# Last two stores of GpSimd on SyncE, the last eviction in two halves, and the last row block stored as two halves

## The chip, the cores and the metric

One core of one Trainium2 chip. The metric is the device time of one execution in microseconds, as the median of several runs.

## The reference

Two heads read inputs of 2048 rows by 1024 columns and their results stand side by side in an output of 2048 x 2048, in bf16.

```
# head A (columns 0 to 1023)
k_shift = sum over t<4 of k[l-(3-t)] * shift_k[:, 3-t]
kv      = k_shift * v
y       = irfft(rfft(kv, 4096) * rfft(ssm_k, 4096))[:2048] + kv * ssm_D
a       = q * y
# head B (columns 1024 to 2047), Lam_bar and B_bar complex, from Lambda, B and log_dt
h[t]    = Lam_bar * h[t-1] + x[t] @ B_bar.T
b       = 2 * Re(h @ C.T) + x * Dskip
out     = concatenate([a, b], axis=-1)
```

## The kernel before

Head A is a convolution done by matmuls with Fourier tables in two levels. Its last stage runs over 16 residues r of the row number: the task `a3.r` multiplies the inverse table `Gt` with `vv` into PSUM, `a3e.r` (ScalarE) evicts that to a tile `ot` of 128 x 1024, `qm.r` (VectorE) multiplies it with q in place, and `ost.r` stores it as two DMAs of 64 rows (128 KB each).

Head B runs over 16 blocks i of 128 rows: `U`, `r1` to `r4`, `sc` and `cm` build the state h, and `y.i.dh.part` (TensorE) multiplies it with the C table into `ps_y`, for the output columns' half dh, 512 columns of f32, in four parts. `ye.i.dh` (ScalarE) evicts a half into the tile `yo` of block i (128 x 1024), and `yst.i` stores that block (256 KB).

The order of all work is written out by hand in the table ORDER. Each word is one task with its arguments; behind a colon stand the buffers that it takes (`b8`: buffer 8 of the ring b, `p0`: bank 0 of PSUM), and behind `@` the engine: `@G` GpSimd, `@S` SyncE, `@D` VectorE. An engine's instructions, and the DMAs that it issues, go in the order of the table. Without `@`, loads are issued by SyncE and stores by GpSimd, and copies run on ScalarE:

```
157    spd = lambda o_, i_: (nc.gpsimd if on[0] == "G" else nc.sync).dma_start(o_, i_)
158    gpd = lambda o_, i_: (nc.sync if on[0] == "S" else nc.gpsimd).dma_start(o_, i_)
```

A framework puts in the waits. Each DMA takes one of eight semaphores in turn, called lanes here (DMAHW0 to 7 for SyncE, DMASW0 to 7 for GpSimd), and a DMA waits until the one before it on its lane has landed. At the end (line 819 of the program, the leaving of the tile context) SyncE waits for every lane, each engine drains, and a barrier of all engines closes the program.

The last row blocks are computed in the order 12, 11, 14, 15, 13, so block 13 is stored last.

Of the kernel before, what the change touches and what calls it, by code (L numbers as in the profile page):

```python
# [127 lines left out]
a3.13:d1 a3.6:d0 a3e.13:b11 vl.3@G:a11 r4.13 a3.5:d2 y.14.0.0:p0 a3e.6:b12 qm.12 y.14.0.1 a3e.5:b2 qm.6 ost.12@S qm.13 y.14.0.2 r3.15:m0 yst.11@S y.14.0.3  # L128
vl.15:a17 a3.8:d1 ye.14.0:b13 ost.13@S a3.7:d0 a3.10:d2 qm.5 a3e.7:b9 y.13.0.0:p0 ost.5 a3e.10:b5 qm.7 y.13.0.1 qm.9 ye.14.1 ost.7 r4.15 y.13.0.2 yst.14@S
ost.6@S y.13.0.3 qm.10 y.15.1.0:p1 ye.13.0:b10 ost.10 a3e.8:b14 a3.11:d0 a3.14:d2 ost.9 a3e.11:b3 qm.8 a3.3:d1 ost.8@S y.15.1.1 a3e.14:b6 qm.11 y.15.1.2 qm.14  # L130
y.15.0.0:p0 ost.11@S ost.14 y.15.0.1 y.15.0.2 a3e.3:b7 a3.15:d0 qm.3 y.15.0.3 a3e.15:b1 y.15.1.3 ye.15.0:b8 qm.15 y.13.1.0:p0 ye.15.1 ost.15 yst.15@S y.13.1.1
ost.3@S y.13.1.2 y.13.1.3 ye.13.1 yst.13@S
"""


def full_kernel(ctx, tc, A_q, A_k, A_v, A_shift_k, A_ssm_k, A_ssm_D, B_x, B_Lre, B_Lim, B_Bre, B_Bim,
# [5 lines left out]
    S, D = A_q.shape[-2], A_q.shape[-1]  # L142
# [3 lines left out]
    T = 128  # L146
# [6 lines left out]
    q, k, v, x = A_q[0], A_k[0], A_v[0], B_x[0]  # L153
    out_a = out[0][:, 0:D]
    out_b = out[0][:, D:2 * D]
    on = [""]
    spd = lambda o_, i_: (nc.gpsimd if on[0] == "G" else nc.sync).dma_start(o_, i_)  # L157
# [43 lines left out]
    st, pools, cms = {}, {}, {}  # L201
# [17 lines left out]
    def rtile(pool, code, name, shape):  # L219
        return pool.tile(shape, BF16, name=name, tag="%s%d" % (code, cur[code].pop(0)), bufs=1)  # L220

    def k2(name, shape=None):
        return rtile(ring, "b", name, shape or [P, D])
# [6 lines left out]
    E = {}  # L230

    def once(key, make):
        if key not in st:
            st[key] = make()
        return st[key]
# [218 lines left out]
    def copy(o_, i_):  # L454
        if on[0] == "D":
            nc.vector.tensor_copy(o_, i_)
        elif on[0] == "G":
            nc.gpsimd.tensor_copy(o_, i_)
        else:
            nc.scalar.copy(o_, i_)  # L460
# [88 lines left out]
    E["ye"] = ye  # L549
    E["yst"] = lambda i: gpd(out_b[i * T:(i + 1) * T, :], st["yo", i][:])  # L550

    def kp(r):
        s0 = (2 * r + 4) % c["kr"]
        spd(st["kring"][:, s0:s0 + 2, :], kr[:, 2 * r:2 * r + 2, :])
# [216 lines left out]
@with_exitstack  # L771
def kernel(
    ctx: ExitStack,
    tc: tile.TileContext,
    A_q: bass.AP,
    A_k: bass.AP,
    A_v: bass.AP,
    A_shift_k: bass.AP,
    A_ssm_k: bass.AP,
    A_ssm_D: bass.AP,  # L780
    B_x: bass.AP,
    B_Lambda_re: bass.AP,
    B_Lambda_im: bass.AP,
    B_B_re: bass.AP,
    B_B_im: bass.AP,
    B_C_re: bass.AP,
    B_C_im: bass.AP,
    B_log_dt: bass.AP,
    B_Dskip: bass.AP,
    out: bass.AP,  # L790
):
    full_kernel(ctx, tc, A_q, A_k, A_v, A_shift_k, A_ssm_k, A_ssm_D, B_x, B_Lambda_re, B_Lambda_im,
                B_B_re, B_B_im, B_C_re, B_C_im, B_log_dt, B_Dskip, out)
# [30 lines left out]
```

## Time and profile before

| | |
|---|---|
| runs, us | 364.92 median of 3 (364.08 to 365.13) |
| profiled execution, us | 361.91 |
| its span, us | 360.0 |
| granted clock of TensorE, mean | 0.987 |
| instructions | 9583 |

The span goes from the first to the last instruction of the profiled execution; the device time of the same execution is 1.9 us longer. The profiled execution is 3.0 us shorter than the median of the runs. In the profile's rows PE is TensorE, DVE is VectorE, ACT is ScalarE, POOL is GpSimd and SP is SyncE; a q behind the name means the engine's sequencer, which waits, drains and issues. A row of the timeline gives the start and the duration in us, the engine, the line of the program, the operation and its tiles, and in brackets how long the engine was idle before it and who ended that. A row of the groups by line ends with the busy time in us, the mean duration in ns, and the idle time before. Lines are those of the kernel before; 819 is the closing line.

### The profile page before, as it was taken

How to read it: one execution, taken by the hardware profiler on the slowest of the kernel's cores; microseconds unless marked ns; L12 is line 12 of the kernel's file. 1: busy time of each engine (PE TensorE's matmuls, PEld its weight loads, DVE VectorE, ACT ScalarE, POOL GpSimd, SP SyncE). 2: the span in 40 equal slices, each digit the busy share in tenths (PEclk: the TensorE clock that was granted, in tenths of full speed). 3: DMA queues.
4: the chain of work that ended last, by engine and by line, in shares of the span. 5: the costliest groups of instructions: out<-in, count | busy, mean ns of one | idle time of the engine just before them, and what ended most of it. 6: DMA issues, size and time to landing. Idle time of an engine off the chain costs nothing.

```text
span 360.0 us, 9583 instructions
## 1 busy us (share of the span) xinstructions
PE 334.4 (93%) x4115; PEld 214.3 (60%) x4115; DVE 319.5 (89%) x260; ACT 259.4 (72%) x332; POOL 63.6 (18%) x112
## 2 busy tenths in 40 slices
PE   3837899999999999999999999999899999999992
PEld 2326687887869966655464656454376479554440
DVE  1999999999999999999789998999799969998730
ACT  2999997989996634675468889888789883453550
POOL 3020261400000012310012120341030310220420
PEclk9998899999999999999999999999999999999998
DMA  8999999799999977598398793999957787989953
GB/s 212 352 319 348 304 349 341 242 273 273 241 332 234 196 192 196 178 319 237 87 186 297 214 255 114 314 334 307 265 195 246 248 259 230 311 277 346 300 157 110
DMA packets 74607, 91.70 MB, mean 255 GB/s; under 512 B 46370, under 2 KB 51762, under 8 KB 74564
## 3 DMA queue, kind: packets, MB, share of 16 engines
q1 hardware_dynamic: 65348, 60.06, 60.1%
q0 software_dynamic: 9216, 31.02, 26.5%
q8 instruction: 32, 0.52, 0.6%
q14 instruction: 11, 0.09, 0.1%
HBM read 47.02 MB, written 33.55 MB: 224 GB/s over the span
## 4 chain that ended last, share of the span: by engine, by line
PE 75%; ACT 10%; DMA 7%; issue 3%; SPq 2%; POOL 1%; DVE 0%; POOLq 0%; ACTq 0%
PE ps_y L538 28%; PE ps_u L483 26%; PE ps_a L679 4%; PE ps_a L709 4%; PE ps_a L645 3%; PE ps_a L611 3%; DMA l2h<-Ys_h 2%; PE ps_a L740 2%; DMA Ys_h<-ysbh 2%; PE ps_t L632 2%; DMA Vs<-vsb 2%; ACT ysb L616 2%; PE ps_y L543 2%; ACT BT L460 2%; SPq L157 1%
## 5 line engine op out<-in xcount | busy, mean ns | idle before, releaser
L483 PEld LDWEIGHTS <-BT 128*128 128x128 bf16 x2048 | 119.2, 98 | 20.9 <-issue 12.5
L483 PE MATMUL ps_u<-xT,BT 128*128 128x128 bf16 x2048 | 125.9, 220 | 4.6 <-ACT BT L460 4.6
L538 PE MATMUL ps_y<-ct,h 128*128 128x512 bf16 x512 | 126.4, 380 | 0.0
L538 PEld LDWEIGHTS <-h 128*128 128x128 bf16 x512 | 44.3, 98 | 55.4 <-issue 14.9
L515 DVE TENSOR_TENSOR_SCAN h<-rtab,h 128x1040 bf16<-128x1040 f32 x32 | 72.5, 2309 | 0.1
L687 ACT CAST s<-ps_a 128x1024 bf16<-128x1024 f32 x64 | 62.6, 1018 | 8.0 <-PE ps_a L679 6.5
L488 ACT CAST u<-ps_u 128x512 bf16<-128x512 f32 x64 | 38.2, 601 | 18.3 <-PE ps_u L483 18.0
L548 ACT CAST yo<-ps_y 128x512 bf16<-128x512 f32 x32 | 18.9, 591 | 33.8 <-PE ps_y L538 29.3
L497 DVE TENSOR_TENSOR mt<-u,Z 128x4096 bf16<-128x4096 bf16 x16 | 36.6, 2289 | 1.8 <-ACT u L488 1.1
L716 ACT CAST vsb<-ps_a 128x1024 bf16<-128x1024 f32 x32 | 31.0, 1017 | 9.9 <-PE ps_a L709 8.4
L497 DVE TENSOR_TENSOR mt<-h,Z 128x4096 bf16<-128x4096 bf16 x16 | 36.6, 2285 | 0.1
L584 DVE TENSOR_TENSOR mt<-kring,wbc 128x2048 bf16<-128x2048 bf16 (+3 forms) x14 | 35.8, 2592 | 0.1
L652 ACT CAST ysbh<-ps_a 128x1024 bf16<-128x1024 f32 x32 | 32.1, 1031 | 4.4 <-PE ps_y L543 2.3
L616 ACT CAST ysb<-ps_a 128x1024 bf16<-128x1024 f32 x32 | 32.3, 1032 | 3.1 <-PE ps_a L645 2.4
L693 DVE TENSOR_TENSOR pq<-s,s 128x2048 bf16<-128x2048 bf16 x16 | 19.5, 1221 | 10.4 <-ACT s L687 10.4
L543 PE MATMUL ps_y<-Dd,xT 128*128 128x128 bf16 x128 | 28.0, 219 | 0.0
L746 ACT CAST ot<-ps_a 128x1024 bf16<-128x1024 f32 x16 | 15.4, 1017 | 7.3 <-PE ps_a L740 4.6
L697 DVE TENSOR_TENSOR s<-s,s 128x2048 bf16<-128x2048 bf16 x16 | 19.5, 1224 | 0.4
L509 DVE TENSOR_TENSOR h<-mt 128x2048 bf16<-128x2048 bf16 x16 | 19.5, 1218 | 0.2
L527 DVE TENSOR_TENSOR h<-mt 128x2048 bf16<-128x2048 bf16 x16 | 19.5, 1218 | 0.2
L543 PEld LDWEIGHTS <-xT 128*128 128x128 bf16 x128 | 12.5, 98 | 11.8 <-issue 0.2
L645 PE MATMUL ps_a<-hT,F1t 128*128 128x512 bf16 x64 | 18.5, 380 | 0.5 <-ACT ysb L616 0.3
(120 smaller groups left out, 320.6 us busy)
## 6 DMA issues: line engine op xcount, KB each, us to landing
Ys_kv<-ysb SPq DMA_DIRECT2D x24, 256.0 KB, 3.9
Ys_h<-ysbh SPq DMA_DIRECT2D x21, 256.0 KB, 3.8
l2h<-Ys_h POOLq DMA_DIRECT2D x10, 512.0 KB, 6.2
vv<-Vs SPq DMA_DIRECT2D x10, 512.0 KB, 7.0
l2k<-Ys_kv SPq DMA_DIRECT2D x9, 512.0 KB, 6.5
Vs<-vsb SPq DMA_DIRECT2D x18, 256.0 KB, 4.7
hk<-in_A_ssm_k_dram SPq DMA_DIRECT2D x8, 512.0 KB, 6.1
kring<-in_A_k_dram SPq DMA_DIRECT2D x7, 512.0 KB, 5.3
```

The source lines that it names most:

```text
L483: nc.tensor.matmul(pu[:, w, jl, :], BT[:, 2 * jp + jl, w, d, :], xT[:, d, :], start=(d == 0), stop=(d == ND - 1))
L488: nc.scalar.copy(u[:, :, 2 * jp:2 * jp + 2, :], st["pu", i, jp][:])
L497: nc.vector.tensor_mul(m, s_, w_)
L515: nc.vector.tensor_tensor_scan(gf, rtab[:].rearrange("p j t -> p (j t)"), gf, 0.0, ALU.mult, ALU.add)
L538: nc.tensor.matmul(py[:], h[:, 1 - w, j, 2:TP], st["CT", dh][:, j, w, :], start=(j == 0 and w == 0), stop=(j == NJ - 1 and w == 1))
L543: nc.tensor.matmul(py[:, dl * P:(dl + 1) * P], st["xT", i][:, d, :], Dd[:, d, :], start=False, stop=False)
L584: nc.vector.tensor_mul(m[:, :, j0:j0 + n, :], a_, wbc[:, j0:j0 + n, :].unsqueeze(1).to_broadcast([P, 2, n, DV]))
L616: nc.scalar.copy(st["ysb", r, u][:], st["pa", r, u][:].rearrange("p e d -> p (e d)"))
L645: nc.tensor.matmul(pd[:, e, :], F1t[:, u, :], st["hT", f, rp][:, e, :], start=True, stop=not sk)
L652: nc.scalar.copy(st["yh", f, rp, u][:], st["pa", f, rp, u][:])
L687: nc.scalar.copy(s16[:, u, :, :], st["ps", key, gq][u][:])
L716: nc.scalar.copy(vsb[:, gi, :].rearrange("p (e d) -> p e d", e=2), st["ps", "v", gq][gi][:])
```

## The change

The stores `ost.14` and `ost.15`, which GpSimd issued, are issued by SyncE, `ost.3` stands ahead of `ost.15` and `yst.15` instead of behind them, the last eviction `ye.13.1` becomes two copies of 256 columns (`yq`), the first on ScalarE, the second on VectorE, and the store `yst.13` becomes two stores of 512 columns (`yh`), the first of which goes ahead of the last matmuls.

```
-y.15.0.0:p0 ost.11@S ost.14 y.15.0.1 ...
+y.15.0.0:p0 ost.11@S ost.14@S y.15.0.1 ...
...
-... y.13.1.0:p0 ye.15.1 ost.15 yst.15@S y.13.1.1
-ost.3@S y.13.1.2 y.13.1.3 ye.13.1 yst.13@S
+... y.13.1.0:p0 ye.15.1 ost.3@S ost.15@S yst.15@S yh.13.0 y.13.1.1
+ y.13.1.2 y.13.1.3 yq.13.1.0 yq.13.1.1@D yh.13.1
...
+    def yh(i, dh):
+        spd(out_b[i * T:(i + 1) * T, dh * 512:(dh + 1) * 512], st["yo", i][:, dh * 512:(dh + 1) * 512])
+    E["yh"] = yh
+
+    def yq(i, dh, v):
+        lo = 512 * dh + 256 * v
+        yo = once(("yo", i), lambda: k2("yo"))
+        copy(yo[:, lo:lo + 256], st["py", i, dh][:, 256 * v:256 * v + 256])
+    E["yq"] = yq
```

The ten new lines move all later line numbers by ten. The end of GpSimd's queue, as a difference; `ot_5499` is the tile of r = 9, `ot_5722` that of r = 14, `ot_5763` that of r = 15:

```order
 L158 DMA out_0_dram<-ot_5499 64x1024 [waits DMASW7_49]
 L158 DMA out_0_dram<-ot_5499 64x1024 [waits DMASW0_49]
-L158 DMA out_0_dram<-ot_5722 64x1024 [waits DMASW1_49,DVE_49]
-L158 DMA out_0_dram<-ot_5722 64x1024 [waits DMASW2_49]
-L158 DMA out_0_dram<-ot_5763 64x1024 [waits DMASW3_49,DVE_49]
-L158 DMA out_0_dram<-ot_5763 64x1024 [waits DMASW4_49]
```

Four DMAs leave, and the two of `ost.9` are GpSimd's last. The end of SyncE's queue before (`ot_5706` is r = 11, `ot_5751` is r = 3, `yo_5769` is block 15, `yo_5688` block 13):

```order
L158 DMA out_0_dram<-ot_5706 64x1024 [waits DMAHW0_49,DVE_49]
L158 DMA out_0_dram<-ot_5706 64x1024 [waits DMAHW1_49]
L158 DMA out_0_dram<-yo_5769 128x1024 [waits DMAHW2_49,Activation_49]
L158 DMA out_0_dram<-ot_5751 64x1024 [waits DMAHW3_49,DVE_49]
L158 DMA out_0_dram<-ot_5751 64x1024 [waits DMAHW4_49]
L158 DMA out_0_dram<-yo_5688 128x1024 [waits DMAHW5_49,Activation_49]
```

And now, behind the two of `ot_5706`:

```order
L158 DMA out_0_dram<-ot_5722 64x1024 [waits DMAHW2_49,DVE_49]
L158 DMA out_0_dram<-ot_5722 64x1024 [waits DMAHW3_49]
L158 DMA out_0_dram<-ot_5751 64x1024 [waits DMAHW4_49,DVE_49]
L158 DMA out_0_dram<-ot_5751 64x1024 [waits DMAHW5_49]
L158 DMA out_0_dram<-ot_5763 64x1024 [waits DMAHW6_49,DVE_49]
L158 DMA out_0_dram<-ot_5763 64x1024 [waits DMAHW7_49]
L158 DMA out_0_dram<-yo_5769 128x1024 [waits DMAHW0_49,Activation_49]
L157 DMA out_0_dram<-yo_5688 128x512 [waits DMAHW1_49]
L157 DMA out_0_dram<-yo_5688 128x512 [waits DMAHW2_49,DVE_49]
```

SyncE issues nine DMAs here instead of four; the last one sits on lane 2 instead of lane 5 and waits for VectorE instead of ScalarE. The end of ScalarE's queue before:

```order
L746 CAST ot_5751<-ps_a_5709 128x1024 [waits PE_49]
L746 CAST ot_5763<-ps_a_5753 128x1024 [waits DMAHW5_49,DMAHW6_49,DVE_49,PE_49]
L548 CAST yo_5769<-ps_y_5730 128x512 [waits DMAHW7_49,PE_49,Activation_49]
L548 CAST yo_5769<-ps_y_5681 128x512 [waits PE_49]
L548 CAST yo_5688<-ps_y_5772 128x512 [waits PE_49]
```

The ends of ScalarE's and then of VectorE's queue now (the copies stand at the line of the helper `copy`):

```order
L756 CAST ot_5751<-ps_a_5709 128x1024 [waits PE_49]
L756 CAST ot_5763<-ps_a_5753 128x1024 [waits DMAHW5_49,DMAHW6_49,DVE_49,PE_49]
L548 CAST yo_5769<-ps_y_5730 128x512 [waits DMAHW7_49,PE_49,Activation_49]
L548 CAST yo_5769<-ps_y_5681 128x512 [waits PE_49]
L460 CAST yo_5688<-ps_y_5772 128x256 [waits PE_49]
```

```order
L760 TENSOR_TENSOR ot_5706<-ot_5706,qt_4607 128x1024 [waits DMAHW1_49,Activation_49]
L760 TENSOR_TENSOR ot_5722<-ot_5722,qt_4765 128x1024 [waits DMAHW2_49,DMASW7_49,DMAHW3_49,DMASW0_49,Activation_49]
L760 TENSOR_TENSOR ot_5751<-ot_5751,qt_4178 128x1024 [waits Activation_49]
L760 TENSOR_TENSOR ot_5763<-ot_5763,qt_4765 128x1024 [waits DMAHW6_49,DMAHW5_49,Activation_49]
L456 CAST yo_5688<-ps_y_5772 128x256 [waits DMASW7_49,DMASW6_49,Activation_49]
```

ScalarE's last copy waits for TensorE, as before; VectorE's new copy reads the same `ps_y_5772` and waits for ScalarE (Activation).

More of the change, by code (lines that the diff above doesn't have):

```diff
@@ L130 @@
 ost.6@S y.13.0.3 qm.10 y.15.1.0:p1 ye.13.0:b10 ost.10 a3e.8:b14 a3.11:d0 a3.14:d2 ost.9 a3e.11:b3 qm.8 a3.3:d1 ost.8@S y.15.1.1 a3e.14:b6 qm.11 y.15.1.2 qm.14
-y.15.0.0:p0 ost.11@S ost.14 y.15.0.1 y.15.0.2 a3e.3:b7 a3.15:d0 qm.3 y.15.0.3 a3e.15:b1 y.15.1.3 ye.15.0:b8 qm.15 y.13.1.0:p0 ye.15.1 ost.15 yst.15@S y.13.1.1
-ost.3@S y.13.1.2 y.13.1.3 ye.13.1 yst.13@S
+y.15.0.0:p0 ost.11@S ost.14@S y.15.0.1 y.15.0.2 a3e.3:b7 a3.15:d0 qm.3 y.15.0.3 a3e.15:b1 y.15.1.3 ye.15.0:b8 qm.15 y.13.1.0:p0 ye.15.1 ost.3@S ost.15@S yst.15@S yh.13.0 y.13.1.1
+ y.13.1.2 y.13.1.3 yq.13.1.0 yq.13.1.1@D yh.13.1
 """
```

## The prediction

> **What bounds the kernel now.** I read the first page for what fills the span, then the chain of work that ended last, and then, since that chain stops before the span does, the closing line of the program (L819) engine by engine.
>
> ```profile
> span 360.0 us, 9583 instructions
> PE 334.4 (93%) x4115; PEld 214.3 (60%) x4115; DVE 319.5 (89%) x260; ACT 259.4 (72%) x332; POOL 63.6 (18%) x112
> PE 75%; ACT 10%; DMA 7%; issue 3%; SPq 2%; POOL 1%; DVE 0%; POOLq 0%; ACTq 0%
> ```
>
> TensorE fills 93% of the span, but the edit touches no matmul. All that it changes lies behind 341 us, so what matters is the end. The last rows of the chain:
>
> ```profile
> 351.10 1.96 PE ps_y L538 x9
> 353.06 0.02 issue
> 353.08 0.59 ACT yo L548
> ```
>
> The last eviction ends at 353.67, and the span at 360.0: the chain says nothing of the last 6.3 us. SyncE's issues by the timeline:
>
> ```profile
> 338.09 0.34 SPq L158 DMA_DIRECT2D out_dram<-yo  x1
> 338.48 6.11 SPq L158 DMA_DIRECT2D out_dram<-ot  x6
> 350.00 0.34 SPq L158 DMA_DIRECT2D out_dram<-yo  x1
> 350.44 1.10 SPq L158 DMA_DIRECT2D out_dram<-ot  x2
> 353.69 0.34 SPq L158 DMA_DIRECT2D out_dram<-yo  x1
> ```
>
> The last store leaves at 353.69. The closing line, asked in pieces from 353 us on (duration in ns as min/median/max, then first and last start in us):
>
> ```profile
> L819 POOLq DRAIN  x1: 8867/8867/8867, 350.3 to 350.3; - x1
> ...
> L819 SPq EVENT_SEMAPHORE  x6: 28/28/187, 354.1 to 354.9; - x6
> ...
> L819 SPq EVENT_SEMAPHORE  x3: 28/28/28, 355.7 to 355.8; - x3
> L819 SPq DRAIN  x2: 7/10/13, 355.9 to 356.0; - x2
> ...
> L819 POOLq EVENT_SEMAPHORE  x4: 17/17/17, 359.2 to 359.9; - x4
> ```
>
> This is the finding. SyncE waits for the landings one lane after another; the last one (the store of 353.69) has landed at 355.7, and SyncE is through at 356.0. GpSimd's drain runs from 350.3 for 8.87 us, to 359.2, and only then does the closing barrier go on, which takes 0.8 us to 360.0. So the last store has 3.2 us of slack (359.2 less 356.0), and GpSimd's drain holds the end.
>
> When does that drain begin? GpSimd's last stores by the timeline:
>
> ```profile
> 340.02 2.08 POOL L158 DMA_DIRECT2D out_dram<-ot  x4 [1.29 <-DVE ot L750]
> 344.66 1.04 POOL L158 DMA_DIRECT2D out_dram<-ot  x2 [2.56 <-DVE ot L750]
> 349.59 0.53 POOL L158 DMA_DIRECT2D out_dram<-ot  x1 [3.89 <-DVE ot L750]
> 350.33 0.53 POOL L158 DMA_DIRECT2D out_dram<-ot  x1 [0.20 <-issue]
> ```
>
> It begins with the last one, at 350.3, and ends 8.3 us behind that store's own end (350.86).
>
> **The change, part by part.**
>
> *ost.14 and ost.15 leave GpSimd: four issues of 0.53 us.* GpSimd's last store is then the fourth of the row at 340.02, which ends at 342.10. With the 8.3 us kept, the drain ends at 350.4. If it keeps an unknown length instead, it may grow by 5.6 us to 356.0 before it shows. The trace has one such drain, so its length after another store isn't shown. From below its price is nothing (the drain leaves the end altogether); from above it is all it has now (the end doesn't move). I take the first, since the drain starts with GpSimd's last issue in the only row there is. Gain: the whole slack, 3.2 us, less what SyncE's own chain gets longer.
>
> *The same four issues on SyncE, and ost.3 ahead of ost.15 and yst.15.* Issues of `ot` there last:
>
> ```profile
> L158 SPq DMA_DIRECT2D out_dram<-ot x8: 467/530/1070, 338.5 to 351.0; - x8
> ```
>
> The products of ost.3 and ost.15 on VectorE, and the sizes of the stores:
>
> ```profile
> 346.97 0.69 DVE L750 TENSOR_TENSOR ot<-ot,qt 128x1024 bf16<-128x1024 bf16 x1 [2.61 <-ACT ot L746]
> 348.61 0.69 DVE L750 TENSOR_TENSOR ot<-ot,qt 128x1024 bf16<-128x1024 bf16 x1 [0.95 <-ACT ot L746]
> ```
> ```profile
> out_dram<-ot SPq DMA_DIRECT2D x13, 128.0 KB, 4.1
> ...
> out_dram<-yo SPq DMA_DIRECT2D x4, 256.0 KB, 3.9
> ```
>
> ost.14, which GpSimd issues at 344.66, goes out behind ost.11 (which ends at 344.59), in a stretch in which SyncE had nothing until 350.00; ost.3 goes out at 347.7, when its product is done, instead of 350.44. Then at 349.3 ost.15 follows with 2 x 0.53, yst.15 and yh.13.0 with 0.34 each: SyncE is free again at 351.1, 2.8 us before the last store is ready. Four times the longest, 1.07, would still end at 353.6. Price 0, covered by the idle SyncE queue. From 349.3 to the last store the data is 640 KB (ost.15, yst.15 and half of yst.13) against 768 KB now (ost.3 besides, without the half), so these transfers end no later.
>
> *The last eviction.* Its rows, on ScalarE and VectorE:
>
> ```profile
> L548 ACT CAST yo<-ps_y 128x512 bf16<-128x512 f32 x32 | 18.9, 591 | 33.8 <-PE ps_y L538 29.3 <-PE ps_a L645 2.9 <-PE ps_y L543 1.5
> ...
> L293 ACT ACTIVATE so<-sv 128x32 f32<-128x32 f32 x1 | 0.2, 229 | 0.0
> ```
> ```profile
> L456 DVE COPY BT<-ps_t 128x1024 bf16<-128x1024 bf16 x2 | 1.4, 692 | 2.0 <-PE ps_t L445 2.0
> ...
> L302 DVE SCALAR_TENSOR_TENSOR tab<-tab 128x1024 f32<-128x1024 f32 x1 | 1.2, 1224 | 0.0
> ...
> L258 DVE CAST p<-ps_t 128x32 f32<-128x32 bf16 x1 | 0.2, 192 | 2.6 <-PE ps_t L253 2.6
> ```
>
> ScalarE: 229 ns at 32 columns and 591 at 512 make 0.75 ns a column, so 256 take 0.40 us (bounds 0.23 and 0.59). VectorE: 192 ns at 32 and 692 at 1024 make 0.50 ns a column, 0.31 us for 256; at the slope of the f32 row (1224 at 1024, 1.04 ns) it would be 0.43. No VectorE row reads f32 out of PSUM, so I take the middle, 0.37 (bounds 0.19 and 0.69).
>
> Do they run side by side? In the changed program VectorE's copy waits for ScalarE's counter and not for TensorE's, though it reads what TensorE wrote; ScalarE's 256-column copy is the instruction that waits for TensorE. So VectorE starts when ScalarE has ended. Such a handover in the timeline:
>
> ```profile
> 347.56 1.01 ACT L746 CAST ot<-ps_a 128x1024 bf16<-128x1024 f32 x1 [0.62 <-PE ps_a L740]
> ```
>
> ScalarE ends at 348.57 and VectorE's product (above) begins at 348.61: 0.04 us. The eviction then takes 0.40 + 0.04 + 0.37 = 0.81 instead of 0.59: 0.22 longer, not shorter. Behind the waiting VectorE copy nothing is queued on its engine; who waits for it is the last half store.
>
> The Trainium skill, "PSUM — Partial Sum Buffer", section "PSUM bank collisions raise a hardware error", has the reason: two engines, ScalarE and VectorE reads included, must not be in one bank on the same partitions at once, disjoint columns or not, and the 512 f32 columns of `ps_y` fill one bank. By that rule the eviction gets 0.22 longer; without it, it would get 0.19 shorter. No run here shows it yet; the program's wait agrees.
>
> The Trainium skill, "VectorE: DVE Perf Modes", section "Why PSUM operands drop a tier", has f32 out of PSUM at one element a cycle, which speaks for the 0.43; the sum would be 0.06 longer.
>
> *The last store is half as long.* Data packets in two windows, one of 0.9 us with the last store alone (2 KB packets), one of 1.0 us with a 256 KB transfer in 1 KB packets:
>
> ```profile
> q1 hardware_dynamic: 144, 0.26, 77.4%
> ```
> ```profile
> q1 hardware_dynamic: 291, 0.27, 77.1%
> ```
>
> 0.9 x 0.774 is 0.70 us on each engine for 256 KB, and 1.0 x 0.771 is 0.77 in the smaller packets; half of the latter is 0.38. So the last store lands 0.32 earlier after its issue (bounds 0, if its length doesn't count, and 0.35, half of the 0.70): 2.0 - 0.3 = 1.7 us.
>
> *SyncE's closing waits.* Nine in all (the rows above), six done by 354.9 and three and two drains from the last landing on, some 0.06 us apart, in the order of the lanes, the semaphores that stores take in turn. The last store moves from lane 5 to lane 2 (more stores ahead of it), so three more waits stand behind it: +0.18 (bounds 0 and 0.3).
>
> **Sum.** SyncE is through at 356.0 + 0.22 - 0.32 + 0.18 = 356.1. The barrier's 0.8 makes 356.9 against 360.0: 3.1 us less. The profiled execution takes 361.91 us, so 358.8; it lies 3.0 below the median of the runs shown (364.92, from 364.08 to 365.13), and I carry the difference over: 364.92 - 3.1 = 361.8. By the bounds together SyncE is through between 355.5 and 357.0, which gives 361.2 to 362.8.
>
> **Rivals.**
>
> *Truly side by side.* The eviction ends after 0.40, 0.41 us sooner than in the sum: 361.4. Against it stands the wait in the program.
>
> *GpSimd's drain doesn't follow its own stores.* It could end 3.2 us behind SyncE's last wait, as it does here (359.2 against 356.0), because it waits for all transfers of the core, or be there only while a profile is taken. Then the end moves with SyncE alone, by +0.1: 365.0, no change. For it: one drain in the trace, and the page doesn't say what ended it. Against it: it starts with GpSimd's last store, and no packet moves in its last 3.8 us, as the busy share of the DMA engines from 353.5 to 360 shows (40 slices of 0.16 us):
>
> ```profile
> DMA  5421116999700000000000000000000000000000
> ```
>
> *SyncE's queue becomes the bound (slower).* The four issues after 349.3 would have to hold back the last store. The end gets 1.1 us later than now only if SyncE is through at 360.3, thus if the last store leaves at 358.1 instead of 353.9; the four would take 8.8 us, 2.2 each, twice the longest row (1.07). At 2.4 each: 366.8. Nothing in the trace is near it.
>
> **How the numbers follow.** 0.3% of 364.92 is 1.1 us, about what a measurement of this kernel can tell from no change. The case of the sum 0.80, side by side 0.06, the drain that stays 0.11, SyncE's queue 0.03. The first two are faster by more than 1.1 us: 0.86; same 0.11; slower 0.03. The first case's bounds with some 0.4 for the spread of the runs make 360.8 to 363.2; toward the drain that stays, partly released, I extend to 363.5, so 360.8 to 363.5.
>
> **What the profile after would show.** GpSimd's drain ending near 350 or 351, and the closing barrier following SyncE's last wait near 356.1; VectorE's 256-column copy starting 0.04 us behind the end of ScalarE's, near 353.5, and ending near 353.9; the last half store landing near 355.6; a span near 356.9. A drain that ends behind 358 us, or a last store that leaves later than 355, would make the prediction wrong.

## The result and the profile after

| | before | after |
|---|---|---|
| runs, us, median | 364.73 (362.25 to 368.64, 20 runs) | 362.04 (360.2 to 368.91, 20 runs) |
| ratio | | 0.9934, 95% interval 0.9906 to 0.9962 |
| profiled execution, us | 361.91 | 362.41 |
| its span, us | 360.0 | 360.6 |
| granted clock, mean | 0.987 | 0.981 |

The kernel got 2.4 us faster (0.9934 of 364.7), between 1.4 and 3.4 by the interval. Here and below the medians take in all runs, the ratios leave out the slow ones, those more than 1.5% above the fastest of their kernel, and of the executions traced only e7's was a slow one. Yet the span of the profiled execution is longer than before's. Where the two differ, a table of three stretches shows: from 60 us to where the two executions run alike again, from there to the start of the last eviction, and from that to the end. Columns: stretch, its length, busy us (and instructions) of TensorE, weight load, VectorE, ScalarE and GpSimd, granted clock, busy share of the DMA engines, GB/s. First before, then after:

```profile
60.00:68.00 8.00, 7.67 (x98) 5.95 (x97) 7.93 (x4) 6.90 (x10) 3.28 (x5) 1.00 0.77 244
68.00:353.08 285.08, 283.29 (x3569) 176.50 (x3566) 259.81 (x176) 202.25 (x250) 46.15 (x83) 1.00 0.85 247
353.08:360.00 6.92, 0.00 (x0) 0.00 (x0) 0.00 (x0) 0.59 (x1) 0.00 (x0) 0.79 0.19 70
```
```profile
60.00:71.20 11.20, 9.65 (x104) 7.54 (x102) 11.03 (x6) 7.76 (x10) 3.77 (x6) 0.85 0.79 262
71.20:356.27 285.07, 283.20 (x3568) 176.40 (x3566) 256.68 (x174) 201.94 (x249) 43.57 (x79) 1.00 0.86 245
356.27:360.60 4.33, 0.00 (x0) 0.00 (x0) 0.42 (x1) 0.37 (x1) 0.00 (x0) 1.00 0.09 30
```

The middle stretch is the same to 0.01 us (285.08 and 285.07). The first is 3.2 us longer in this execution. Instruction by instruction, ScalarE runs 0.3 us late at 40 us, 1.6 from 60.4 on and 3.2 at 68.5 us (times of before). The step at 60.4 is a wait for a DMA that ScalarE doesn't have there before, at a granted clock of 1.00 in both:

```profile
62.04 1.01 ACT L626 CAST ysb<-ps_a 128x1024 bf16<-128x1024 f32 x1 [1.13 <-DMA Ys_h<-ysbh]
```

The last 1.6 us come where the granted clock is 0.85 on the mean instead of 1.00: the trace has it at 0.5 for 3.4 us from 64.7 us on. The change touches nothing there, and such windows fall elsewhere in other executions (near 260 us in e1 and e4 below); I take this for the scatter of the body, which the medians average. The last stretch is what the change edits: 6.9 us before, 4.4 after (the window above stops at 360.60, 0.05 us short of the end). I call it the tail. It is 2.5 us shorter (6.88 and 4.37), and that is the gain of the medians, 2.4 to 2.7, within the interval.

The tail in the timeline (start, duration, engine, line, operation):

```profile
356.27 0.37 ACT L460 CAST yo<-ps_y 128x256 bf16<-128x256 f32 x1 [3.11 <-PE ps_y L538]
356.68 0.42 DVE L456 CAST yo<-ps_y 128x256 bf16<-128x256 f32 x1 [4.19 <-ACT yo L460]
357.13 0.33 SPq L157 DMA_DIRECT2D out_dram<-yo  x1
```

ScalarE's half ends at 356.65, and VectorE starts 0.03 us behind it, released by ScalarE (the bracket). GpSimd's last stores:

```profile
343.21 2.08 POOL L158 DMA_DIRECT2D out_dram<-ot  x4 [1.29 <-DVE ot L760]
```

And the closing line, L829 now, again in pieces (duration in ns as min/median/max, then first and last start in us):

```profile
L829 POOLq DRAIN  x1: 8768/8768/8768, 344.5 to 344.5; - x1
...
L829 SPq EVENT_SEMAPHORE  x6: 28/28/28, 359.0 to 359.3; - x6
...
L829 SPq DRAIN  x2: 7/10/13, 359.3 to 359.4; - x2
...
L829 POOLq EVENT_SEMAPHORE  x4: 17/17/17, 359.4 to 360.5; - x4
...
L829 POOLq DRAIN  x2: 108/146/184, 359.6 to 360.2; - x2
L829 POOLq EVENT_SEMAPHORE_RANGE_CLEAR  x1: 141/141/141, 359.7 to 359.7; - x1
```

GpSimd's drain now starts at 344.5, 0.25 us ahead of the last of `ost.9`'s stores (344.76), and is over at 353.3, 6 us before SyncE is through at 359.4. SyncE holds the end, as forecast: the last store has landed at 359.0, 0.4 us of waits follow, then the barrier, which takes 1.2 us to 360.6 instead of 0.8.

### The profile page after: what moved, and what is told of

The parts are those of the page before. It is cut to its first block, busy times and chain, and to the rows that moved or that the text cites. A ratio compares the mean times of both kernels' runs of the same rounds, so it can differ in the third digit from the quotient of the medians.

```text
span 360.6 us, 9586 instructions
## 1 busy us (share of the span) xinstructions
PE 337.3 (94%) x4115; PEld 216.5 (60%) x4115; DVE 320.0 (89%) x261; ACT 259.4 (72%) x332; POOL 61.5 (17%) x108
## 4 chain that ended last, share of the span: by engine, by line
PE 74%; issue 10%; DVE 6%; DMA 6%; POOL 2%; ACT 1%; SPq 1%; POOLq 0%; DVEq 0%; ACTq 0%
PE ps_y L538 28%; PE ps_u L483 27%; PE ps_a L689 4%; PE ps_a L719 4%; PE ps_a L655 3%; PE ps_a L621 3%; DMA Ys_h<-ysbh 2%; DMA l2h<-Ys_h 2%; PE ps_a L750 2%; PE ps_y L543 2%; PE ps_t L642 1%; DVE mt L594 1%; DMA praw<-in_B_Dskip_dram 1%; DVE pq L703 1%; DVE s L707 1%
## 5 line engine op out<-in xcount | busy, mean ns | idle before, releaser
L483 PEld LDWEIGHTS <-BT 128*128 128x128 bf16 x2048 | 120.6, 99 | 20.9 <-issue 12.4
L483 PE MATMUL ps_u<-xT,BT 128*128 128x128 bf16 x2048 | 127.4, 222 | 4.6 <-ACT BT L460 4.6
L655 PE MATMUL ps_a<-hT,F1t 128*128 128x512 bf16 x64 | 19.5, 400 | 1.6 <-ACT ysb L626 1.6
```

What stands on the lines that cost most here:

```text
L483: nc.tensor.matmul(pu[:, w, jl, :], BT[:, 2 * jp + jl, w, d, :], xT[:, d, :], start=(d == 0), stop=(d == ND - 1))
L655: nc.tensor.matmul(pd[:, e, :], F1t[:, u, :], st["hT", f, rp][:, e, :], start=True, stop=not sk)
```

## Experiments

Two theories stood against mine (GpSimd's drain held the end, and moving its start is the whole gain): that the halved eviction and store bring the gain, and that SyncE's queue does, each store moved to it bringing a part. The body scatters by some us from run to run, so each verdict rests on the tail of the profiled execution, with the medians beside it. Times are us; "drain ends" (GpSimd's long drain) and "SyncE through" (the end of its two closing drains, as in the prediction) count from the start of the last eviction, and the barrier runs from the later of the two to the end; these and the tail are from one trace each. The totals of e9 to e11 are single runs and carry no verdict.

| kernel | median (runs) | ratio to before, 95% | tail | drain ends | SyncE through | barrier |
|---|---|---|---|---|---|---|
| before | 364.73 (20) | | 6.88 | +6.1 | +2.90 | 0.79 |
| after | 362.04 (20) | 0.9934 (0.9906 to 0.9962) | 4.37 | -3.0 | +3.15 | 1.23 |
| e1_stores_only | 360.40 (6) | 0.9847 (0.9798 to 0.9895) | 4.37 | -3.0 | +3.15 | 1.22 |
| e2_halves_only | 365.84 (12) | 1.0011 (0.9971 to 1.0050) | 6.88 | +6.1 | +2.96 | 0.79 |
| e3_only_15_moved | 362.75 (10) | 0.9954 (0.9910 to 0.9997) | 3.90 | +0.8 | +2.78 | 1.12 |
| e4_only_14_moved | 367.29 (12) | 1.0037 (0.9996 to 1.0078) | 6.86 | +5.7 | +2.78 | 1.15 |
| e5_after_again | 361.82 (12) | 0.9964 (0.9921 to 1.0006) | 4.36 | -3.0 | +3.14 | 1.22 |
| e6_stores_only_again | 361.69 (12) | 0.9917 (0.9872 to 0.9962) | 4.38 | -3.0 | +3.15 | 1.23 |
| e7_two_banks | 362.62 (12) | 0.9914 (0.9866 to 0.9962) | 3.68 | -3.0 | +2.46 | 1.22 |
| e8_lane_seven | 361.21 (12) | 0.9913 (0.9872 to 0.9954) | 2.91 | -6.7 | +2.14 | 0.77 |
| e9_late_gpsimd_copy | 365.54 (1) | | 6.27 | +5.2 | +3.15 | 1.11 |
| e10_six_memsets | 369.42 (1) | | 3.93 | -2.9 | +3.16 | 0.78 |
| e11_one_eviction_two_stores | 362.31 (1) | | 4.13 | -3.0 | +2.90 | 1.23 |

The kernel before had a median of 365.50 beside e1 to e4, 365.29 beside e5 to e8, and 366.19 (one run) beside e9 to e11. The diffs below are against the kernel after, in the table ORDER.

### The stores alone

```
-... ost.3@S ost.15@S yst.15@S yh.13.0 y.13.1.1 y.13.1.2 y.13.1.3 yq.13.1.0 yq.13.1.1@D yh.13.1
+... ost.3@S ost.15@S yst.15@S y.13.1.1 y.13.1.2 y.13.1.3 ye.13.1 yst.13@S
```

> Only the stores move (ost.14 and ost.15 to SyncE, ost.3 ahead of ost.15); the last eviction is one copy and yst.13 one store, as before. The stretch from the start of the last eviction to the end of the span was 6.9 us before and 4.3 after the whole change. Theory 1, GpSimd's drain held the end: the stretch is 4.0 to 4.4 us (0.59 eviction, 2.0 store, 0.5 closing waits, 0.8 to 1.2 barrier), and the time is 2 to 3 us under before, as with the whole change. Theory 2, the halves of the eviction and the store made the gain: 6.9 us, no gain. Theory 3, stores are done sooner by SyncE's queue than by GpSimd's, each moved one a part of it: about 5.5 us.

The last eviction in the timeline, and GpSimd's drains in the closing line (the longest of the three is the one; it starts first):

```profile
355.17 0.59 ACT L547 CAST yo<-ps_y 128x512 bf16<-128x512 f32 x1 [3.11 <-PE ps_y L537]
```
```profile
L828 POOLq DRAIN  x3: 107/184/8763, 343.4 to 359.1; - x3
```

The span is 359.5, so the tail is 4.37, as in the kernel after: the moved stores bring the whole gain of the tail. The total is 5.6 us under before (0.9847), more than the 2 to 3 expected; e6 runs this kernel again.

### The halves alone

```
-... ost.11@S ost.14@S ... ye.15.1 ost.3@S ost.15@S yst.15@S yh.13.0 y.13.1.1 y.13.1.2 ...
+... ost.11@S ost.14 ... ye.15.1 ost.15 yst.15@S y.13.1.1 ost.3@S yh.13.0 y.13.1.2 ...
```

> Only the halves: ost.14 and ost.15 stay on GpSimd, the last eviction is two copies of 256 columns on ScalarE and VectorE, yst.13 two stores. Theory 1: the drain still ends 8.8 us behind its start with ost.15's second DMA, so the stretch from the last eviction's start to the end stays at 6.9 us and the time at that of before. Theory 2: 4.3 us, and 2 to 3 us less time.

The halves of the eviction, and the closing line:

```profile
356.24 0.37 ACT L459 CAST yo<-ps_y 128x256 bf16<-128x256 f32 x1 [3.11 <-PE ps_y L537]
356.65 0.42 DVE L455 CAST yo<-ps_y 128x256 bf16<-128x256 f32 x1 [4.19 <-ACT yo L459]
```
```profile
L828 SPq DRAIN  x2: 7/10/13, 359.1 to 359.2; - x2
...
L828 POOLq DRAIN  x1: 8870/8870/8870, 353.5 to 353.5; - x1
```

SyncE is through at 359.2, GpSimd's drain ends at 353.5 + 8.87 = 362.4, and the span at 363.1. The tail is before's 6.9. The halves bring nothing, and the theory that they do falls.

### Each of the two stores alone

Here ost.15 alone goes to SyncE, with one eviction and one last store:

```
-... ost.11@S ost.14@S ... ye.15.1 ost.3@S ost.15@S yst.15@S yh.13.0 y.13.1.1 ...
+... ost.11@S ost.14 ... ye.15.1 ost.15@S yst.15@S y.13.1.1 ost.3@S ... ye.13.1 yst.13@S
```

> Of the whole change only ost.15 goes to SyncE; ost.14 stays on GpSimd and is its last store, 8 us ahead of the last eviction. Theory 1: the drain of 8.8 us begins 7.9 us before the last eviction and ends 0.9 behind its start, long before SyncE is through: the stretch is 4.0 to 4.4 us, the whole gain. Theory 3: half the gain of e1.

And here ost.14 alone:

```
-... ost.11@S ost.14@S ... ye.15.1 ost.3@S ost.15@S yst.15@S yh.13.0 y.13.1.1 ...
+... ost.11@S ost.14@S ... ye.15.1 ost.15 yst.15@S y.13.1.1 ost.3@S ... ye.13.1 yst.13@S
```

> Of the whole change only ost.14 goes to SyncE; ost.15 stays on GpSimd as its last store. Theory 1: the drain starts with ost.15 as before, the stretch from the last eviction to the end stays at 6.9 us, no gain. Theory 3: half the gain of e1.

GpSimd's last stores in e3, and its drain:

```profile
350.12 1.04 POOL L157 DMA_DIRECT2D out_dram<-ot  x2 [2.58 <-DVE ot L759]
```
```profile
L828 POOLq DRAIN  x1: 8778/8778/8778, 350.5 to 350.5; - x1
```

The same in e4:

```profile
352.88 1.05 POOL L157 DMA_DIRECT2D out_dram<-ot  x2 [7.50 <-DVE ot L759]
```
```profile
L828 SPq DRAIN  x2: 7/10/13, 359.1 to 359.1; - x2
L828 POOLq DRAIN  x1: 8782/8782/8782, 353.3 to 353.3; - x1
```

In e3 the last eviction starts at 358.53 (its span is 362.4); the drain ends at 359.3, and SyncE is through at 361.3, so SyncE holds the end; the tail is 3.9, a little under the 4.0 to 4.4 expected, since SyncE is through 0.37 us sooner behind the eviction's start than in e1 (the lane of the last store, see below) and the barrier is 0.1 shorter. In e4 GpSimd still has ost.15 (last eviction at 356.37, span 363.2); its drain ends at 362.1, 2.9 us behind SyncE, and the tail is 6.9. The drain is as long in both (8.78) and starts with GpSimd's last store (to 0.1 us); only where that store stands decides. The theory of SyncE's queue falls too: e4 has ost.14 on SyncE and gains nothing, and e3 has the gain with ost.3 behind yst.15, as before.

### The kernel after and the stores alone, side by side

e1's ratio (0.9847) lay below after's (0.9934). Both were run again, beside each other, unchanged.

> The changed kernel once more, beside e6, on one chip. By theory 1 its end is e6's: the stretch from the last eviction's start to the end of the span is 4.3 to 4.4 us in both, so their times differ only by how often the clock is halved, and the two ratios to the kernel before overlap. By the rival, that the halves of the eviction and the store cost something beside the tail, it stays some 3 us slower than e6, as the first runs of the two had it.

> The kernel of e1 once more, beside the changed kernel: stretch 4.4 us, time 2 to 3 us under before.

The tails are again equal at 4.4 (4.36 and 4.38; 4.37 in both first traces), and the intervals of the ratios, 0.9964 and 0.9917, overlap. That of e5 takes in 1: by the totals of this set alone, the kernel after isn't clearly faster than before. I take the difference of the totals as the body's scatter; a difference below about 0.5% between the two isn't excluded.

### Two PSUM banks

The last 512 columns are computed as two groups of 256 in a bank each (`yw`), so that the first can be evicted (`yv`, ScalarE) while TensorE fills the second; the stores (`yu`) take columns 0 to 767 and 768 to 1023.

```
-... y.13.1.0:p0 ye.15.1 ost.3@S ost.15@S yst.15@S yh.13.0 y.13.1.1 ... yq.13.1.0 yq.13.1.1@D yh.13.1
+... yw.13.0:p0 ye.15.1 ost.3@S ost.15@S yst.15@S yw.13.1:p1 yv.13.0 yu.13.0.768 yv.13.1 yu.13.768.1024
...
+                nc.tensor.matmul(py[:], h[:, 1 - w, j, 2:TP], st["CT", 1][:, j, w, 256 * hf:256 * hf + 256],
+                                 start=(j == 0 and w == 0), stop=(j == NJ - 1 and w == 1))
```

> As the changed kernel, but the last 512 columns are computed as two groups of 256 in two PSUM banks, each evicted by ScalarE, so that the first eviction runs beside the second group's matmuls; the last store is 256 columns (64 KB), the one before it 768. If eviction and store are what is left of the tail: the last eviction takes 0.37 us instead of 0.83, the store lands 1.7 us after its issue, closing waits 0.45, barrier 1.2 to 1.3: a stretch of 3.8 us against 4.4. TensorE's time for the block is the same if two matmuls of 256 columns take as long as one of 512. If the landing is a fixed time and the smaller rows of 512 B are slow: 4.0 to 4.1.

The last eviction:

```profile
360.81 0.37 ACT L459 CAST yo<-ps_y 128x256 bf16<-128x256 f32 x1 [1.49 <-PE ps_y L566]
```

The span ends at 364.5: the tail is 3.7, 0.7 less than after's. TensorE isn't slower for twice the matmuls at half the width: from the start of `ye.15.1` to that of the last eviction it is 3.73 us, against 3.69 before. The last store of 64 KB lands 1.59 us after its issue.

### The last store on the last lane

e7, and the stores of ost.9 and ost.10 go to SyncE as well; block 13 goes out in three stores, which puts the last on lane 7 (DMAHW7).

```
-... ost.10 ... ost.9 ... yst.15@S yh.13.0 y.13.1.1 ...
+... ost.10@S ... ost.9@S ... yst.15@S yh.13.0 yw.13.1:p1 yv.13.0 yu.13.512.768 yv.13.1 yu.13.768.1024
```

> As e7, with ost.9 and ost.10 on SyncE too and block 13 stored in three pieces (512, 256, 256 columns), so that the last store takes the last lane (DMAHW7) and no lane is waited for behind it. If the order of the closing waits costs what the changed kernel showed (0.45 us behind the landing on lane 2, 0.26 on lane 5 before): SyncE is through 0.1 to 0.2 us behind the landing, and the stretch is 3.4 to 3.5 us. If the lanes don't matter: 3.8 as e7.

The last eviction and the closing line:

```profile
356.92 0.37 ACT L459 CAST yo<-ps_y 128x256 bf16<-128x256 f32 x1 [1.49 <-PE ps_y L566]
```
```profile
L848 SPq EVENT_SEMAPHORE  x2: 28/28/28, 358.5 to 358.9; - x2
...
L848 SPq DRAIN  x1: 13/13/13, 359.0 to 359.0; - x1
```

The store lands at 358.9 and SyncE is through 0.15 us later instead of 0.45. The span is 359.8, the tail 2.9, the shortest of all, 1.5 below after's. It is 0.5 under the 3.4 to 3.5 expected: against e7 the lane gives the 0.3 foreseen, and besides the barrier takes 0.77 us instead of 1.22, because a pause is missing from it (see the six memsets below). The median, 361.21, can't be told from e5's 361.82: the intervals overlap.

### A late GpSimd instruction that is no store

Does the drain hang on stores? One copy of 16 columns by GpSimd, behind `ye.15.1`, whose result nobody uses:

```
-... yst.15@S yh.13.0 ...
+... yst.15@S gl.15 yh.13.0 ...
+        nc.gpsimd.tensor_copy(t[:], st["yo", i][:, 512:528])
```

> The changed kernel with one more instruction on GpSimd: a copy of 16 columns that waits for block 15's last eviction, 3.1 us ahead of the last eviction's start; nothing reads its result. GpSimd's last store is still ost.9, 8.4 us earlier. If the 8.8 us belong to the software DMAs (counted from the last one, or until they are all done): the drain begins behind the copy, takes well under 1 us, the stretch stays at 4.3 us (3.9 to 4.4). If any last instruction of GpSimd brings a drain of 8.8 us: it ends 5.7 us behind the last eviction's start and the stretch is 6.5 to 6.9 us, as before the change.

GpSimd's last instructions, and the closing line:

```profile
344.44 2.08 POOL L157 DMA_DIRECT2D out_dram<-ot  x4 [1.29 <-DVE ot L764]
354.46 0.20 POOL L563 COPY gl<-yo 128x16 bf16<-128x16 bf16 x1 [7.93 <-ACT yo L547]
```
```profile
L833 SPq DRAIN  x2: 7/10/13, 360.6 to 360.7; - x2
L833 POOLq DRAIN  x1: 8223/8223/8223, 354.4 to 354.4; - x1
```

GpSimd's last stores had gone out by 346.5, 8 us before the copy. Still a drain of 8.2 us follows the copy, to 362.7, 2.0 us behind SyncE, and the tail is 6.3 (last eviction at 357.51, span 363.8). So the drain needs no store just issued: it follows GpSimd's last instruction, a copy as well as a store. The tail is 0.2 under the 6.5 to 6.9 expected, because this drain is 0.55 us shorter than after's (8.77). What sets the length isn't shown; behind a store it is 8.29 in e8 and 8.54 in e10.

### Six more GpSimd instructions

The barrier takes 1.2 us after and 0.8 before. Is that because SyncE comes last now? In the trace, the barrier after has a pause of 0.35 us on GpSimd between the clearing of the semaphores (359.7) and the next drain (360.2), behind GpSimd's 196th recorded instruction, and that drain takes 0.18 us instead of 0.05; before has six more GpSimd instructions, and there that number falls ahead of the long drain. Six memsets far ahead of the end make up for them:

```
-... ost.0 y.11.0.2 ...
+... ost.0 gm y.11.0.2 ...
+        for n in range(6):
+            nc.gpsimd.memset(t[:, n, :], 0.0)
```

> The changed kernel with six memsets on GpSimd in an idle stretch near 325 us, into a tile that nothing reads. The closing barrier took 0.8 us before and 1.3 after the change; in the traces GpSimd has a gap of 0.35 to 0.4 us behind its 196th instruction, which lies inside the barrier where GpSimd runs 199 to 202 instructions, and ahead of its drain where it runs 205. If the gap hangs on the place in GpSimd's program: with 205 instructions again it falls ahead of the drain, the barrier takes 0.8 us and the stretch 3.9 us. If the barrier is longer because SyncE comes last: 1.3 and 4.3 to 4.4 us, as after the change.

The barrier on GpSimd, by the closing line:

```profile
L835 POOLq EVENT_SEMAPHORE  x4: 17/17/17, 366.9 to 367.6; - x4
L835 POOLq DRAIN  x2: 51/80/108, 367.1 to 367.4; - x2
L835 POOLq EVENT_SEMAPHORE_RANGE_CLEAR  x1: 139/139/139, 367.2 to 367.2; - x1
```

The pause is gone from between the clearing and the second drain, and the barrier takes 0.78 us although SyncE comes last (the tail is 3.9). The table has the converse: in e4 and e9 GpSimd comes last, as in the kernel before, but with 202 and 200 recorded instructions, and the barrier takes 1.15 and 1.11 us. So the longer barrier hangs on the count of GpSimd's instructions and not on who is last. In the nine traces in which the 196th falls into the barrier, a pause of 0.33 to 0.36 us stands behind it; in before and e2 GpSimd idles 0.2 us there, ahead of its last store, in e10 less than 0.1, and e8 ends with its 194th and has no such pause. What it is the traces don't show. The total of this one run (369.42) says nothing: its body had a granted clock of 0.976, and its tail is shorter than after's.

### One eviction, two stores

```
-... y.13.1.3 yq.13.1.0 yq.13.1.1@D yh.13.1
+... y.13.1.3 ye.13.1 yh.13.1
```

> The changed kernel, but the last eviction is one ScalarE copy of 512 columns, and block 13 is still stored as two halves. The eviction takes 0.59 instead of 0.83 us, all else as after: the stretch is 4.1 us (4.37 - 0.24). Against e1 (4.37, one store): the half store lands 0.2 sooner, and one lane less is waited for behind it, 4.37 - 0.26 = 4.1. If the two copies do run side by side in part, the stretch is 4.4 or more.

```profile
356.42 0.58 ACT L547 CAST yo<-ps_y 128x512 bf16<-128x512 f32 x1 [3.11 <-PE ps_y L537]
```

The span ends at 360.6; the tail is 4.13, against 4.37 after. Halving the eviction costs 0.24 us; the shorter store wins it back.

## Why the prediction was right, point by point

Forecast was 361.8 us, measured 362.04, within the range. The tail was forecast 3.1 us shorter and is 2.5 us shorter. That the totals lie only 0.2 us apart is thus in part luck: the median of the kernel before alone was 364.73, 365.50 and 365.29 in three sets of runs.

- **GpSimd's drain held the end, and SyncE had 3.2 us of slack.** Shown: e1 and e3, in which the drain ends early, have the gain; e2 and e4, in which it ends 5.7 to 6.1 us behind the eviction's start, have none. The rival in which the drain doesn't follow its own stores (it ends some fixed time behind SyncE) falls with the same runs. Whether the drain is there without a profile, the other half of that rival, isn't shown: each run on record after the change has a span and a granted clock beside its time.
- **The drain's end with 8.3 us kept, near 350 or 351.** It ended at 353.3 in an execution that runs 3.2 us late, thus at 350.1 on before's clock. Right in its place, but the reason was too narrow: the step ties the drain to GpSimd's stores, and e9 shows it behind a 0.2 us copy.
- **SyncE's queue, price 0.** SyncE issues the first half store of block 13 at 354.3, 2.8 us before the last store, which leaves 0.03 us behind VectorE's copy. On before's clock the first is issued at 351.1, 0.4 us later than worked out, which leaves the price at 0. The slower rival falls.
- **The eviction, 0.40 + 0.04 + 0.37 = 0.81.** Measured 0.373 + 0.032 + 0.425 = 0.83, with VectorE at the slope of the f32 row and not at the middle that I took. The Trainium skill, "VectorE: DVE Perf Modes", section "Why PSUM operands drop a tier", has one element a cycle for f32 from PSUM; the copy's 425 ns for 256 columns agree, as they lie on that row's slope of 1.04 ns a column. The rival with both engines side by side falls. The Trainium skill, "PSUM — Partial Sum Buffer", section "PSUM bank collisions raise a hardware error", forbids it; the trace agrees as far as it goes (0.03 us between the two), but there the program's own wait keeps them apart, and reading one bank at once wasn't tried, since by that section dropping the wait would bring a collision. e11 prices the halving at 0.24, as worked out (0.22).
- **The half store, 0.32 sooner.** It lands 1.84 us after its issue instead of 2.03: 0.19. Its packets take about half the time on each engine, as worked out, as the DMA rows of a window of 0.8 us around it show (0.8 x 0.482 is 0.39 us, before 0.70):

```profile
q1 hardware_dynamic: 144, 0.13, 48.2%
```

  Only 0.2 of the 0.3 saved there reaches the landing.
- **The closing waits, +0.18.** Right: from the landing to the end of SyncE's drains it is 0.26 us before and 0.45 after. The runs show that one lane costs 0.06. With a whole last store SyncE is through 2.78 us behind the eviction's start on lane 7 (e3), 2.90 on lane 5 (before) and 3.15 on lane 1 (e1).
- **The barrier, 0.8.** This is the term that was mis-sized: it is 1.23 us. It makes 0.44 of the 0.6 us that the tail lacks; the half store makes 0.13 and the eviction 0.02. It was carried over from the profile before as if it were fixed. There the clearing of the semaphores (359.5) and the drain behind it (359.7) follow each other closely:

```profile
L819 POOLq DRAIN  x3: 51/99/8867, 350.3 to 359.7; - x3
L819 POOLq EVENT_SEMAPHORE_RANGE_CLEAR  x1: 141/141/141, 359.5 to 359.5; - x1
```

  But a pause of 0.35 us, which stands at one place in GpSimd's program, moved in between them when GpSimd lost six recorded instructions, the four stores and two semaphore waits (e10 takes it out again), and the drain behind it takes 0.13 longer.
- **The profiled execution against the median.** The sum was made against one execution, and its distance to the median was carried over. The span after (360.6) misses the forecast (356.9) by 3.7, of which 3.2 came before 71 us, 1.6 of it where the clock was at half speed for 3.4 us. So the last store, too, leaves at 357.1 us, later than the 355 that the prediction named as a sign of being wrong; without those 3.2 us it is 353.9, as forecast. The Trainium skill, "TensorE: Matmul & The Clock Gate", section "🔬 Part 1: The HAM clock gate (the "warmup" mystery)", has the gate work in windows of about 3.4 us that run freely; the trace agrees with the length. A span of one execution can't show a gain of 2.5 us here; a tail can.

## What to carry to other kernels

The chain of work stops at the last computation: what follows is read from the closing line, engine by engine, and the engine that is through last is the one to relieve. On GpSimd that means its last instruction, a store or a copy, should start some 9 us before the others are through; moving another store (e4) or splitting the last eviction (e2) gains nothing while its drain holds the end. Then the tail is made of the last eviction, the last store's landing, its lane and the barrier. In e8 it went from 4.4 to 2.9: 0.7 by two PSUM banks with a 64 KB last store (e7), 0.3 by the last lane and 0.45 by the shorter barrier. The medians can't tell that gain from the scatter.

## What the runs showed of the hardware

- GpSimd's closing drain takes 8.2 to 8.9 us in all 13 traces, and its row begins 0.02 to 0.26 us ahead of GpSimd's last instruction, a store as well as a copy of 0.2 us, 8 us behind the last store of GpSimd (e9). A program in which GpSimd issues no DMA at all wasn't tried.
- A pause of about 0.35 us stands behind GpSimd's 196th recorded instruction in the nine traces in which that number falls into the barrier; where it falls ahead of the long drain (before, e2, e10) or isn't reached (e8), the barrier is 0.3 to 0.45 us shorter. What it is, no run here shows.
- From issue to landing at the end: 256 KB 2.03 us, 128 KB 1.84, 64 KB 1.59.
- The granted clock falls to 0.5 in windows of 3.4 us, at times two in a row, whose number and place differ between the traces (up to 71 us two in before and four in after; e1 and e4 have one near 260 us). The one at 64.7 us in after cost 1.6 us. The 285 us from there to the last eviction repeat to 0.01 between before and after.
